# A list-scheduled attention stage: its weight conversions as three vector steps, its table of dates and one tile's path replaced

## The chip, the cores and the metric

The kernel runs on one core of one Trainium2 chip. The metric is the device time of one execution in microseconds (us). The median of three runs before the change is 1078.47 us, and the runs lie between 1077.97 and 1079.72 us. The core has five engines with a queue each: PE (matmul; PEld is its weight load), DVE (vector), ACT (scalar activation), POOL (GpSimd) and SP, which here only issues DMAs. Each works through its queue in order.

## The reference

Three layers follow each other. The first is an attention over 4 batches of 8 heads, 576 positions and 64 channels, whose scores more than tau below the maximum of their row are dropped:

```python
scores = scale * np.matmul(q, k.transpose(0, 1, 3, 2))
thresh = np.max(scores, axis=-1, keepdims=True) - tau
scores = np.where(scores >= thresh, scores, -1000000000.0)
attn = np.exp(scores - np.max(scores, axis=-1, keepdims=True))
x = np.matmul(attn / attn.sum(-1, keepdims=True), v)      # then heads side by side: 2304 x 512
g = x @ w_gate                                            # 512 x 1536
x = (g * sigmoid(g) * (x @ w_val)) @ w_out                # 1536 x 512
out = ((x @ w1) * (x @ w2) @ w3) @ w_out2                 # d_ff 1024
```

The weights arrive as 64-bit floats. The chip reads them as pairs of 32-bit words, and each block of 128 x 512 numbers has to be converted before it can be used.

## The kernel before

**Precision.** Every fp32 operand of a matmul is split into a rounded part (hi) and a rest (lo), and products are sums of two or three matmuls. So every tile that comes out of a matmul is evacuated from PSUM twice.

**Attention.** The heads are taken in 16 pairs (p), each with 9 score tiles (i) of 128 x 576. For a tile n, PE multiplies into one of two buffers `s_bank` (L627). DVE reads it twice: E with the row minimum (L659) and the mask into P (L675, which needs E's statistic). ACT takes a small bias step (L668) and the exponential (L684). The matmul of tile n needs the mask of tile n-2, since there are two buffers. Then P is transposed on PE (L591) into one of four `t_bank` buffers, in ten tiles per pair, and each of them is split into hi and lo in `AT` or `ATL` along a path that a letter of `ROWS` gives:

- Y: ACT copies the bank to `tmp` (L801), POOL rounds it (L371) and subtracts (L376). Seven of the ten tiles.
- X: ACT rounds from the bank (L814), DVE subtracts (L818).
- Z: ACT rounds (L814), PE subtracts the rounded part in the bank by a product with minus the identity (L598, function `less`), ACT copies the rest (L825).

The value products (L869, L881) use these tiles. Besides this, each pair transposes and splits the q and k of the next (`khi`, `klo`, `qhi`, `qlo`, L736 and L742), and POOL splits v (`sp`). Every fourth pair POOL also splits leftover rows of q and k (`qkls`) and of v (`VLZ`).

**Weight conversions in attention.** In pairs 3, 6 and 9 (`EARLY`) one block of weights is converted on the side by `plan_conv`. DVE separates the mantissa (L412, L415, L418: three instructions in one step called `begin`), ACT makes the power of two from the exponent (L426, L427), POOL subtracts (L432), DVE forms the value (L444), ACT rounds it (L481) and POOL or DVE takes the rest (L485). The raw weights are fetched by SP (L401), in `begin`, in `value` and in a step of their own.

**What sets the order.** `Plan` is a list scheduler that runs when the program is built. Every step has an engine, two costs (`busy`, how long it holds its engine, and `until`, when its result is there), the steps that it depends on, and a due date in units of score tiles. `Plan.order` puts, engine by engine, the step that can start first, and among those that could start together the one with the earliest date. The dates are offsets from the pair's first tile, taken from the table `W`; `W["two"]` pulls the odd tile of two forward. The result is a fixed order of instructions; nothing is decided on the chip. At the end of attention a second planner (`Program`, from the function `ending` on) orders the last pair and all that follows, beginning from the times at which the first plan ended.

**After attention** come the blocks of `x` and the dense layers, nearly all of it matmuls on L1524 and L1724.

Of the kernel before, what the change touches and what calls it, by code (L numbers as in the profile page):

```python
# [11 lines left out]
I32 = mybir.dt.int32  # L12
U16 = mybir.dt.uint16
ACTF = mybir.ActivationFunctionType
ALU = mybir.AluOpType
# [17 lines left out]
EARLY = (3, 6, 9)  # L33


ROWS, LAST = ("YXYYYXYYYZ",), "XXYZ"

W = {
    "s": 1.84, "two": 0.59, "exp": -0.21, "bias": 2.86, "k": 0.01, "q": 0.5, "left": 4.95,
# [3 lines left out]
}  # L43


# [254 lines left out]
def kernel(  # L300
# [17 lines left out]
    nc = tc.nc  # L318
# [13 lines left out]
    f32 = lambda ap: ap.bitcast(F32)  # L332
# [28 lines left out]
    def tmp(dt=F32):  # L361
        return stg.tile([P, 512], dt, tag="tmp", name="tmp", bufs=N_TMP)
# [21 lines left out]
    wide = 2 if w_gate.dtype == mybir.dt.int64 else 1  # L384
# [19 lines left out]
    def conv_mantissa(raw):  # L404

        if wide == 1:
            return raw
        two = raw.rearrange("p (n t) -> p n t", t=2)
        a, x = two[:, :, 0], two[:, :, 1]
        low = raw.bitcast(U16).rearrange("p (n t) -> p n t", t=4)[:, :, 1]  # L410
        m = tmp(I32)
        nc.vector.tensor_scalar(  # L412
            out=m, in0=x, scalar1=(1 << 20) - 1, scalar2=None, op0=ALU.bitwise_and
        )
        nc.vector.tensor_scalar(  # L415
            out=x, in0=x, scalar1=-(1 << 20), scalar2=None, op0=ALU.bitwise_and
        )
        nc.vector.scalar_tensor_tensor(  # L418
            out=f32(m), in0=low, scalar=2.0 ** -16, in1=m, op0=ALU.mult, op1=ALU.add
        )  # L420
        return a, m, x
# [50 lines left out]
    conv_in, conv_raw, conv_mid = deque(), deque(), deque()  # L472
# [48 lines left out]
    def attention(actx):  # L521
# [6 lines left out]
        ld = lctx.enter_context(tc.tile_pool(name="ld", bufs=2))  # L528
# [184 lines left out]
        plan = Plan()  # L713
# [405 lines left out]
        def plan_conv(due, engine, deps):  # L1119
            k, r = {}, plan.res("tmp")  # L1120

            def begin():
                conv_fetch()
                k["raw"], *k["rest"] = conv_raw.popleft()
                k["bits"] = conv_mantissa(k["raw"])

            def value():
                conv_fetch()
                k["val"] = conv_value(k["bits"])

            def copy():
                k["lo"] = k["rest"][0](k["val"], later=True)

            ld = plan.add("SP", 0.55, 5.0, deps, conv_fetch, due - 4)
            a = plan.add("DVE", 2.8, 2.9, [ld], begin, due, opens=r)
            c = plan.add("ACT", 1.5, 1.65, [a], lambda: conv_power(k["bits"]), due + 0.2)
            d = plan.add("POOL", 1.0, 1.05, [c], lambda: conv_less(k["bits"]), due + 0.4)
            e = plan.add("DVE", 1.0, 1.1, [d], value, due + 1)
            f = plan.add("ACT", 0.47, 0.6, [e], copy, due + 1.2)
            plan.add(engine, 1.25, 1.3, [f], lambda: k["lo"](), due + 1.4, closes=r)  # L1140

# [2 lines left out]
        def make_plan():  # L1144
            score, tops, mask, ex = {}, {}, {}, {}
            es, pv, ready, left_done = {}, {}, {}, {}
            ready[0], second, first_read, lefts[0], vls[0] = plan_start()
            for p in range(NP):
                z = p * NTILE
                tail_pair = p == NP - 1  # L1150
                for i in range(NTILE if not tail_pair else 2):
                    n = z + i
                    deps = [mask.get(n - 2)] + ready[p]
                    if i == 0:
                        deps = deps + [u for t in range(NTILE) for u in pv.get(("T", p - 2, t), [])]
                    if i >= 4 and p == 0:
                        deps = deps + second
                    big = (1.06 if i == 4 else 0.53)

                    def go(n=n):  # L1160
                        banks[n] = mm_scores(*tiles[n])

                    score[n] = plan.add("PE", big, big + 0.17, deps, go, n - W["s"])
                    if tail_pair:
                        continue
                    war = pv.get(("T", p - 2, i), [])

                    def mx(n=n):
                        es[n] = el_max(*tiles[n], banks[n])

                    two = n - n % 2 * W["two"]
                    a = plan.add("DVE", 0.68, 0.91, [score[n]], mx, two)
                    tops[n] = a
                    mask[n] = plan.add(
                        "DVE", 0.73, 0.82, [a] + war,
                        lambda n=n, p=p, i=i: el_mask(p, i, banks.pop(n), es.pop(n)), two + 0.2)
                    group = next(g for g in SETS if i in g)
                    if i != group[-1]:
                        continue
                    c = plan.add(  # L1180
                        "ACT", 0.16, 0.3, [tops[z + j] for j in group],
                        lambda p=p, group=group: el_bias(p, group), n + W["bias"])
                    for j in group:
                        ex[z + j] = plan.add(
                            "ACT", 0.77, 0.79, [mask[z + j], c], lambda p=p, j=j: el_exp(p, j),
                            z + j + W["exp"])
                if tail_pair:
                    break
                if p + 2 < NP:
# [5 lines left out]
                    ld = plan.add("SP", 1.4, 5.0, [mask[z - 1]] if p else [first_read], loads, z)  # L1195
                    landed[p + 2, 0] = landed[p + 2, 1] = ld
                q = p + 1
# [19 lines left out]
                for c in range(4):  # L1217
                    a, e = plan_T(
                        p, z + W["T0"] + W["t0"] * c, row[c], P0, old[:2],
                        lambda c=c, p=p: [pbuf[p, t][:, c * P:(c + 1) * P] for t in range(4)],  # L1220
                        (AT[0][:, 0, c, 0:512], AT[0][:, 1, c, 0:512]))
# [3 lines left out]
                a, lq = plan_T(  # L1225
                    p, z + W["lq"], row[4], [ex[z + 4]], old,
                    lambda p=p: [pbuf[p, 4][:, c * P:(c + 1) * P] for c in range(4)],
                    tuple(ATT[:, :, e, :, 512:S].rearrange("p h c q -> p c h q") for e in range(2)),
                    "p (c h q) -> p c h q")
                uses[4] += a  # L1230
                a, co = plan_corner(p, z + W["co"], [ex[z + 4]], old)
                uses[4] += a
                late = p == NP - 2
                if late:
# [3 lines left out]
                a, kl = plan_T(  # L1238
                    p, z + W["kl"], row[5], P0 + P1, old,
                    lambda p=p: [pbuf[p, t][:, 512:640] for t in range(4)],  # L1240
                    (ATL[:, 0, 0:512], ATL[:, 1, 0:512]))
# [749 lines left out]
    for f in range(PLAIN, NF1):  # L1991
# [3 lines left out]
        one, two = (seven(pair, f, "gv", True, h_dram, "h") for pair in range(2))  # L1995
# [122 lines left out]
    for c in range(NF2 // 2):  # L2118
        t = whole_back(c, -14.0 + 2 * c, first)
# [63 lines left out]
    for at, j in enumerate(order):  # L2183
        c0, n = blocks[j]
# [3 lines left out]
        for t in range(n // P):  # L2188
            bank, a = buf("T"), buf("tmp")
# [57 lines left out]
```

## Time and profile before

| | |
|---|---|
| median of the runs | 1078.47 us (1077.97 to 1079.72) |
| the profiled execution, its own time | 1076.61 us |
| its span, first to last instruction | 1074.8 us |
| PE busy | 1044.9 us, 97% |
| weight loads on PE (PEld) | 910.8 us, 85% |
| DVE | 846.2 us, 79% |
| ACT | 638.7 us, 59% |
| POOL | 285.7 us, 27% |
| mean granted TensorE clock | 0.995 of full speed |

The shares are averages over stages that differ. POOL has almost no work after the first 345 us, and it is the attention stage, up to about 295 us, where all four engines are nearly full at once. There a stage's own rows must be read, not the page's totals.

### The profile page before, as it was taken

The page shows a single profiled execution, that of the slowest core. Times are in us where ns is not written, and L with a number is a line of the kernel's source. Part 1 is how long each engine was busy: PE and PEld are TensorE (multiplying, and loading weights), DVE is VectorE, ACT ScalarE, POOL GpSimd, SP SyncE. Part 2 cuts the span into 40 slices and gives each one's busy share as a digit, 9 for nine tenths or more (in the row PEclk, how much of TensorE's full clock was granted, in tenths as well). Part 3 has the DMA queues.
Part 4 walks back from the last instruction along what each step waited for, and adds up shares of the span by engine and source line. Part 5 has one row for each costly group of instructions (what it writes and reads, how often), then busy time and mean ns, then how long its engine had stood idle before and what let it go on. Part 6 is the DMA issues. An engine that isn't in the chain of part 4 may idle for free.

```text
span 1074.8 us, 16990 instructions
## 1 busy us (share of the span) xinstructions
PE 1044.9 (97%) x5830; PEld 910.8 (85%) x5830; DVE 846.2 (79%) x1551; ACT 638.7 (59%) x1353; POOL 285.7 (27%) x307
## 2 busy tenths in 40 slices
PE   7998989999999999999999999999999999999998
PEld 6998989899877888888888889878888888888886
DVE  8999999999997969999999975976977776442320
ACT  6998989999874546665667654544433444232220
POOL 5899898998854000000000000000000000000000
PEclk9999999999999999999999999999999999999999
DMA  7686866776557124545457661461222325621531
GB/s 181 162 213 172 195 157 161 202 169 155 161 168 255 39 94 161 183 152 206 152 182 238 225 232 41 159 232 40 83 84 89 123 92 193 240 79 52 152 121 49
DMA packets 127206, 162.37 MB, mean 151 GB/s; under 512 B 48688, under 2 KB 83312, under 8 KB 127120
## 3 DMA queue, kind: packets, MB, share of 16 engines
q1 hardware_dynamic: 126976, 161.29, 49.4%
q8 instruction: 46, 0.75, 0.3%
q14 instruction: 40, 0.33, 0.1%
q10 hardware_dynamic: 144, 0.00, 0.0%
HBM read 93.47 MB, written 44.19 MB: 128 GB/s over the span
## 4 chain that ended last, share of the span: by engine, by line
PE 78%; DVE 12%; ACT 5%; issue 2%; DMA 2%; SPq 1%; POOL 0%; DVEq 0%; ACTq 0%
PE t_bank L1524 26%; PE t_bank L1724 16%; PE s_bank L1724 11%; PE s_bank L627 6%; PE s_bank L1524 6%; PE t_bank L591 5%; PE t_bank L869 4%; DVE slot L1564 2%; ACT P L684 1%; DVE P L675 1%; DVE E L659 1%; DMA x_dram<-xs 1%; PE t_bank L881 1%; DMA slot<-v_dram 1%; DVE slot L1620 1%
## 5 line engine op out<-in xcount | busy, mean ns | idle before, releaser
L1524 PE MATMUL t_bank<-slot,slot 128*128 128x512 f32 (+1 forms) x1680 | 340.7, 362 | 2.4 <-DVE slot L1564 2.4
L1524 PEld LDWEIGHTS t_bank<-slot,slot 128*128 128x128 f32 x1680 | 285.5, 190 | 53.1 <-DVE slot L1564 4.3
L1724 PE MATMUL t_bank<-slot,slot 128*128 128x512 f32 x816 | 196.8, 390 | 0.6 <-ACT tmp L1743 0.6
L1564 DVE TENSOR_TENSOR slot<-slot,slot 128x512 fp32r<-128x512 f32 (+1 forms) x247 | 158.5, 677 | 40.2 <-ACT slot L2015 28.0
L1724 PEld LDWEIGHTS t_bank<-slot,slot 128*128 128x128 f32 x816 | 152.1, 188 | 32.0 <-ACT tmp L1743 1.4
L1724 PE MATMUL s_bank<-slot,slot 128*128 128x512 f32 x612 | 147.0, 389 | 0.0
L376 POOL TENSOR_TENSOR AT<-tmp,AT 128x512 fp32r<-128x512 f32 x105 | 137.4, 1308 | 8.5
L1724 PEld LDWEIGHTS s_bank<-slot,slot 128*128 128x128 f32 x612 | 114.9, 188 | 23.8
L1743 ACT COPY tmp<-t_bank 128x512 f32<-128x512 f32 x102 | 59.4, 583 | 114.2 <-PE t_bank L1724 114.0
L675 DVE SCALAR_TENSOR_TENSOR P<-s_bank,stat,E 128x576 f32<-128x576 f32 x144 | 114.4, 811 | 2.0
L684 ACT ACTIVATE P<-P,stat 128x576 f32<-128x576 f32 x144 | 112.1, 779 | 3.9 <-DVE P L675 1.6
L659 DVE TENSOR_SCALAR_CACHE_REDUCE E<-s_bank,tau_sb 128x576 f32<-128x576 f32 x135 | 107.0, 810 | 7.4 <-PE s_bank L627 7.1
L1572 ACT CAST slot<-slot 128x512 fp32r<-128x512 f32 x135 | 81.0, 621 | 52.9 <-DVE slot L1564 19.5
L627 PE MATMUL s_bank<-R,L 128*128 128x288 f32 x512 | 95.5, 313 | 13.4 <-DVE P L675 12.3
L627 PEld LDWEIGHTS s_bank<-R,L 128*128 128x128 f32 x512 | 73.1, 190 | 19.3 <-issue 13.1
L591 PE MATMUL t_bank<-ident,P 128*128 128x128 f32 x640 | 88.7, 279 | 0.0
L1524 PE MATMUL s_bank<-slot,slot 128*128 128x512 f32 (+1 forms) x432 | 84.7, 354 | 0.0
L1524 PEld LDWEIGHTS s_bank<-slot,slot 128*128 128x128 f32 x432 | 71.5, 189 | 11.3
L591 PEld LDWEIGHTS t_bank<-ident,P 128*128 128x128 f32 x640 | 76.1, 144 | 2.2 <-DVE AT L1310 0.4
L426 ACT ACTIVATE raw<-raw,ebias 128x512 int32<-128x512 int32 x76 | 58.9, 775 | 30.7 <-DVE slot L1614 30.7
L2015 ACT CAST slot<-slot 128x512 fp32r<-128x512 f32 (+1 forms) x100 | 52.7, 577 | 37.4 <-DMA slot<-h_dram 32.7
L869 PE MATMUL t_bank<-AT,sp 128*128 128x288 f32 x448 | 73.9, 298 | 0.0
(157 smaller groups left out, 1330.9 us busy)
## 6 DMA issues: line engine op xcount, KB each, us to landing
slot<-h_dram SPq DMA_DIRECT2D x40, 512.0 KB
h_dram<-h SPq DMA_DIRECT2D x34, 512.0 KB
raw<-in_moe_w_dram SPq DMA_DIRECT2D x32, 512.0 KB
raw<-in_moe_w_out_dram SPq DMA_DIRECT2D x20, 512.0 KB
x_dram<-xs SPq DMA_DIRECT2D x64, 144.0 KB
L<-qlo SPq DMA_DIRECT2D x60, 128.0 KB
L<-qhi SPq DMA_DIRECT2D x60, 128.0 KB
raw<-in_moe_w_gate_dram SPq DMA_DIRECT2D x12, 512.0 KB
```

The costliest lines, as they stand in the source:

```text
L376: nc.gpsimd.tensor_tensor(out=lo, in0=src, in1=f32(hi), op=ALU.subtract)
L591: nc.tensor.matmul(bank[:, t * P:(t + 1) * P], lhsT=part, rhs=ident, is_transpose=True, start=(t == 0), stop=(t == len(parts) - 1),)
L627: nc.tensor.matmul(o, lhsT=lhs, rhs=R[:, c:c + HALF], start=(h == hs2[0] and e == 0), stop=(h == hs2[-1] and e == 1),)
L659: nc.vector.tensor_scalar(out=halves(t), in0=sb[:, :, 0:HALF], scalar1=tau_sb, scalar2=None, op0=ALU.add, op1=ALU.min, accum_out=st[:, 0, c],)
L675: nc.vector.scalar_tensor_tensor(out=halves(p_tile(p, i)), in0=sb[:, :, 0:HALF], scalar=st[:, 0, c], in1=halves(t), op0=ALU.is_gt, op1=ALU ...
L684: nc.scalar.activation(out=u, in_=u, func=ACTF.Exp, scale=-FAR, bias=st[:, 1, c], accum_out=sums[p // HP][:, c],)
L869: nc.tensor.matmul(b["t"][:, 0:HALF], lhsT=splits[p, 2][:, 4 * h + c, :, :].rearrange("p a d -> p (a d)"), rhs=AT[h][:, e, c, cs], start=( ...
L1524: nc.tensor.matmul(o, lhsT=lhs(a), rhs=rhs(c), start=(first and i == 0), stop=(last and i == 2))
L1564: nc.vector.tensor_tensor(out=out, in0=x, in1=y, op=ALU.subtract)
L1572: act(lambda: nc.scalar.copy(out=un["t"][:, 0, :], in_=src()), [key], [(un, 0)], 0.52, due, after)
L1724: nc.tensor.matmul(ap(), lhsT=un["t"][:, a, (off + kk) * P:(off + kk + 1) * P], rhs=x[kk]["ap"](c), start=(start and kk == 0 and i == 0), ...
L1743: act(lambda: nc.scalar.copy(out=k[n]["t"], in_=xa()), [(x, 0)], [(k[n], 0)], 0.47, NOW)
```

## The change

`ROWS` puts the second of the ten tiles on path Z, where it was on X. The table `W` gets other numbers throughout. `plan_conv` splits its first step into three with dates 0.05 apart, so that the scheduler can set other steps between them, and gives the value step a larger cost. The score step on DVE (`mx`) gets larger costs too. The instructions of a conversion are the same as before, with new line numbers for the mantissa (L1131, L1138, L1145).

```diff
-ROWS, LAST = ("YXYYYXYYYZ",), "XXYZ"
+ROWS, LAST = ("YZYYYXYYYZ",), "XXYZ"
 W = {
-    "s": 1.84, "two": 0.59, "exp": -0.21, "bias": 2.86, "k": 0.01, "q": 0.5, "left": 4.95,
+    "s": 1.87, "two": 0.47, "exp": 0.37, "bias": 4.36, "k": -1.1, "q": 0.82, "left": 4.25,
...
             def begin():
                 conv_fetch()
-                k["raw"], *k["rest"] = conv_raw.popleft()
-                k["bits"] = conv_mantissa(k["raw"])
+                raw, *k["rest"] = conv_raw.popleft()
...
+                    nc.vector.tensor_scalar(
+                        out=m, in0=x, scalar1=(1 << 20) - 1, scalar2=None, op0=ALU.bitwise_and
+                    )
+
+            def high():
...
+                    nc.vector.tensor_scalar(
+                        out=x, in0=x, scalar1=-(1 << 20), scalar2=None, op0=ALU.bitwise_and
+                    )
+
+            def low():
...
+                    nc.vector.scalar_tensor_tensor(
+                        out=f32(m), in0=k["low"], scalar=2.0 ** -16, in1=m,
+                        op0=ALU.mult, op1=ALU.add,
+                    )
...
-            a = plan.add("DVE", 2.8, 2.9, [ld], begin, due, opens=r)
+            a = plan.add("DVE", 0.7, 0.8, [ld], begin, due, opens=r)
+            a = plan.add("DVE", 0.6, 0.7, [a], high, due + 0.05)
+            a = plan.add("DVE", 1.2, 1.3, [a], low, due + 0.1)
             c = plan.add("ACT", 1.5, 1.65, [a], lambda: conv_power(k["bits"]), due + 0.2)
             d = plan.add("POOL", 1.0, 1.05, [c], lambda: conv_less(k["bits"]), due + 0.4)
-            e = plan.add("DVE", 1.0, 1.1, [d], value, due + 1)
+            e = plan.add("DVE", 1.3, 1.4, [d], value, due + 1)
...
-                    a = plan.add("DVE", 0.68, 0.91, [score[n]], mx, two)
+                    a = plan.add("DVE", 0.73, 1.02, [score[n]], mx, two)
```

What this does to the queues is seen at three places. The first is DVE in the first conversion (pair 3). Before, from the mantissa (L412) to the value (L444):

```order
L412 TENSOR_SCALAR tmp<-raw 128x512
L415 TENSOR_SCALAR raw<-raw 128x512
L418 SCALAR_TENSOR_TENSOR tmp<-raw,tmp 128x512
L659 TENSOR_SCALAR E,stat<-s_bank,tau_sb 128x576
L818 TENSOR_TENSOR AT<-t_bank,AT 128x512
L675 SCALAR_TENSOR_TENSOR P_1022<-s_bank,stat,E 128x576
L659 TENSOR_SCALAR E,stat<-s_bank,tau_sb 128x576
L675 SCALAR_TENSOR_TENSOR P_1023<-s_bank,stat,E 128x576
L659 TENSOR_SCALAR E,stat<-s_bank,tau_sb 128x576
L675 SCALAR_TENSOR_TENSOR P_1024<-s_bank,stat,E 128x576
L444 SCALAR_TENSOR_TENSOR tmp<-tmp,raw 128x512
```

After, the first of the three mantissa steps (L1131) and what follows it:

```order
L1131 TENSOR_SCALAR tmp<-raw 128x512
L818 TENSOR_TENSOR ATL<-t_bank,ATL 128x512
L659 TENSOR_SCALAR E,stat<-s_bank,tau_sb 128x576
L742 SCALAR_TENSOR_TENSOR qlo<-t_bank,q_scale,qhi 128x512
L675 SCALAR_TENSOR_TENSOR P_1018<-s_bank,stat,E 128x576
L659 TENSOR_SCALAR E,stat<-s_bank,tau_sb 128x576
```

and behind that the other two (L1138, L1145), up to the value:

```order
L1138 TENSOR_SCALAR raw<-raw 128x512
L675 SCALAR_TENSOR_TENSOR P_1019<-s_bank,stat,E 128x576
L1145 SCALAR_TENSOR_TENSOR tmp<-raw,tmp 128x512
L659 TENSOR_SCALAR E,stat<-s_bank,tau_sb 128x576 x2
L675 SCALAR_TENSOR_TENSOR P_1015<-s_bank,stat,E 128x576
L675 SCALAR_TENSOR_TENSOR P_1016<-s_bank,stat,E 128x576
L659 TENSOR_SCALAR E,stat<-s_bank,tau_sb 128x576
L444 SCALAR_TENSOR_TENSOR tmp<-tmp,raw 128x512
```

Five steps of other work now stand between the first two mantissa steps and one between the last two. Between the last of them and the value stand five instructions (two of them in one row), where seven stood before.

The second place is ACT in the same conversion. Before, from the exponential of the tile whose mask stands just ahead of the mantissa (P_1026) to the two powers (L426, L427):

```order
L684 ACTIVATE P_1026,sums<-P_1026,stat 128x576
L894 COPY xs<-t_bank 128x288
L801 COPY tmp<-t_bank 128x512
L814 CAST AT<-t_bank 128x512
L801 COPY tmp<-t_bank 128x512 x2
L426 ACTIVATE raw<-raw,ebias 128x512
L427 ACTIVATE raw<-raw,ebias 128x512
```

After, from the exponential of the tile whose mask stands just ahead of the last mantissa step (P_1019):

```order
L684 ACTIVATE P_1019,sums<-P_1019,stat 128x576
L426 ACTIVATE raw<-raw,ebias 128x512
L427 ACTIVATE raw<-raw,ebias 128x512
L801 COPY tmp<-t_bank 128x512
L814 CAST AT<-t_bank 128x512
L801 COPY tmp<-t_bank 128x512
```

The powers now follow that exponential at once; a value copy (L894) and four evacuations stood between before. On POOL the subtraction L432 stands behind the split of v (`sp`) now, where it stood between the round and the subtraction of a tile.

The third place is DVE in a pair without a conversion (the last pair but two, behind its `qlo`). Before:

```order
L659 TENSOR_SCALAR E,stat<-s_bank,tau_sb 128x576 x2
L675 SCALAR_TENSOR_TENSOR P_4016<-s_bank,stat,E 128x576
L675 SCALAR_TENSOR_TENSOR P_4017<-s_bank,stat,E 128x576
L659 TENSOR_SCALAR E,stat<-s_bank,tau_sb 128x576 x2
L675 SCALAR_TENSOR_TENSOR P_4013<-s_bank,stat,E 128x576
L675 SCALAR_TENSOR_TENSOR P_4014<-s_bank,stat,E 128x576
L818 TENSOR_TENSOR AT<-t_bank,AT 128x512
L659 TENSOR_SCALAR E,stat<-s_bank,tau_sb 128x576 x2
L675 SCALAR_TENSOR_TENSOR P_4015<-s_bank,stat,E 128x576
L675 SCALAR_TENSOR_TENSOR P_4016<-s_bank,stat,E 128x576
L659 TENSOR_SCALAR E,stat<-s_bank,tau_sb 128x576
L675 SCALAR_TENSOR_TENSOR P_4306<-s_bank,stat,E 128x576
```

After:

```order
L675 SCALAR_TENSOR_TENSOR P_4013<-s_bank,stat,E 128x576
L659 TENSOR_SCALAR E,stat<-s_bank,tau_sb 128x576
L675 SCALAR_TENSOR_TENSOR P_4014<-s_bank,stat,E 128x576
L659 TENSOR_SCALAR E,stat<-s_bank,tau_sb 128x576
L675 SCALAR_TENSOR_TENSOR P_4010<-s_bank,stat,E 128x576
L659 TENSOR_SCALAR E,stat<-s_bank,tau_sb 128x576
L675 SCALAR_TENSOR_TENSOR P_4011<-s_bank,stat,E 128x576
L659 TENSOR_SCALAR E,stat<-s_bank,tau_sb 128x576
L675 SCALAR_TENSOR_TENSOR P_4012<-s_bank,stat,E 128x576
L659 TENSOR_SCALAR E,stat<-s_bank,tau_sb 128x576
L675 SCALAR_TENSOR_TENSOR P_4013<-s_bank,stat,E 128x576
L659 TENSOR_SCALAR E,stat<-s_bank,tau_sb 128x576
```

E and P of single tiles alternate now where two E stood ahead of two P, and the subtraction L818 into AT is gone (it is L598 on PE and L825 on ACT now). The last 935 rows of PE's queue, the dense layers, are the same in both.

## Rows read from the trace of the kernel before

**Rows 1.** Windows: start:end, length, busy (count) PE, PEld, DVE, ACT, POOL, PEclk, DMA.
```profile
20.00:285.00 265.00, 251.75 (x1933) 242.32 (x1930) 252.34 (x489) 245.00 (x650) 240.17 (x259) 0.99 0.71 173
253.35:270.53 17.18, 17.18 (x137) 16.75 (x136) 16.22 (x34) 16.47 (x45) 14.90 (x16) 1.00 0.64 151
345.00:1074.00 729.00, 723.53 (x3492) 610.42 (x3492) 525.60 (x937) 342.48 (x593) 1.38 (x2) 1.00 0.40 137
```
**Rows 2.** Instructions of tile qlo: min/median/max ns, first and last start.
```profile
L742 DVE SCALAR_TENSOR_TENSOR qlo<-t_bank,q_scale,qhi x15: 730/741/752, 14.0 to 270.5; 128x512 fp32r<-128x512 f32 x15
```
**Rows 3.** Timeline of DVE, qlo: start us, us, line [idle before <-releaser].
```profile
66.65 0.74 DVE L742 SCALAR_TENSOR_TENSOR qlo<-t_bank,q_scale,qhi 128x512 fp32r<-128x512 f32 x1
...
85.72 0.75 DVE L742 SCALAR_TENSOR_TENSOR qlo<-t_bank,q_scale,qhi 128x512 fp32r<-128x512 f32 x1
...
107.09 0.73 DVE L742 SCALAR_TENSOR_TENSOR qlo<-t_bank,q_scale,qhi 128x512 fp32r<-128x512 f32 x1
...
141.86 0.73 DVE L742 SCALAR_TENSOR_TENSOR qlo<-t_bank,q_scale,qhi 128x512 fp32r<-128x512 f32 x1
...
164.29 0.74 DVE L742 SCALAR_TENSOR_TENSOR qlo<-t_bank,q_scale,qhi 128x512 fp32r<-128x512 f32 x1
...
253.35 0.73 DVE L742 SCALAR_TENSOR_TENSOR qlo<-t_bank,q_scale,qhi 128x512 fp32r<-128x512 f32 x1
...
270.53 0.74 DVE L742 SCALAR_TENSOR_TENSOR qlo<-t_bank,q_scale,qhi 128x512 fp32r<-128x512 f32 x1
```
**Rows 4.** Timeline of all engines in the first conversion, 70 to 86 us.
```profile
70.23 0.97 DVE L412 TENSOR_SCALAR tmp<-raw 128x512 int32<-128x512 int32 x1
...
71.67 1.21 DVE L418 SCALAR_TENSOR_TENSOR tmp<-raw,tmp 128x512 f32<-128x512 uint16 x1
...
78.58 1.03 POOL L432 TENSOR_TENSOR raw<-raw 128x512 int32<-128x512 int32 x1
...
79.64 1.74 DVE L444 SCALAR_TENSOR_TENSOR tmp<-tmp,raw 128x512 f32<-128x512 f32 x1 [1.33 <-POOL raw L432]
...
83.86 2.04 PE L627 MATMUL s_bank<-R,L 128*128 128x288 f32 x8 [3.81 <-DVE P L675]
```
**Rows 5.** Timeline of DVE and POOL in the second and third conversion.
```profile
128.40 1.77 DVE L418 SCALAR_TENSOR_TENSOR tmp<-raw,tmp 128x512 f32<-128x512 uint16 x1
...
135.47 1.04 POOL L432 TENSOR_TENSOR raw<-raw 128x512 int32<-128x512 int32 x1
...
186.84 0.68 DVE L418 SCALAR_TENSOR_TENSOR tmp<-raw,tmp 128x512 f32<-128x512 uint16 x1
...
192.08 1.04 POOL L432 TENSOR_TENSOR raw<-raw 128x512 int32<-128x512 int32 x1
```
**Rows 6.** Timeline of DVE in a pair without a conversion.
```profile
260.46 0.69 DVE L818 TENSOR_TENSOR AT<-t_bank,AT 128x512 fp32r<-128x512 f32 x1
261.07 0.81 DVE L659 TENSOR_SCALAR_CACHE_REDUCE E<-s_bank,tau_sb 128x576 f32<-128x576 f32 x1
...
261.80 0.82 DVE L659 TENSOR_SCALAR_CACHE_REDUCE E<-s_bank,tau_sb 128x576 f32<-128x576 f32 x1
...
266.27 0.82 DVE L659 TENSOR_SCALAR_CACHE_REDUCE E<-s_bank,tau_sb 128x576 f32<-128x576 f32 x1 [0.16 <-PE s_bank L627]
...
267.13 0.82 DVE L675 SCALAR_TENSOR_TENSOR P<-s_bank,stat,E 128x576 f32<-128x576 f32 x1
```
**Rows 7.** Timeline of ACT and PE in the same pair.
```profile
266.76 0.59 ACT L801 COPY tmp<-t_bank 128x512 f32<-128x512 f32 x1 [0.38 <-PE t_bank L591]
267.24 0.61 ACT L736 ACTIVATE khi<-t_bank 128x512 fp32r<-128x512 f32 x1
...
254.25 0.49 PE L598 MATMUL t_bank<-AT,minus_r 128*128 128x512 f32 x1
254.59 1.22 PE L869 MATMUL t_bank<-AT,sp 128*128 128x288 f32 x8
```
**Rows 8.** Waits of POOL, 20 to 300 us: us in total, times, longest us.
```profile
POOL AT L371 <- ACT tmp L801: 16.1, 8, 6.2
```

More of the change, by code (lines that the diff above doesn't have):

```diff
@@ L1123, in begin @@
                 conv_fetch()
-                k["raw"], *k["rest"] = conv_raw.popleft()
-                k["bits"] = conv_mantissa(k["raw"])
+                raw, *k["rest"] = conv_raw.popleft()
+                k["bits"] = raw
+                if wide == 2:
+                    two = raw.rearrange("p (n t) -> p n t", t=2)
+                    k["low"] = raw.bitcast(U16).rearrange("p (n t) -> p n t", t=4)[:, :, 1]
+                    k["bits"] = two[:, :, 0], tmp(I32), two[:, :, 1]
+                    _, m, x = k["bits"]
+                    nc.vector.tensor_scalar(
+                        out=m, in0=x, scalar1=(1 << 20) - 1, scalar2=None, op0=ALU.bitwise_and
+                    )
+            def high():
+                if wide == 2:
+                    x = k["bits"][2]
+                    nc.vector.tensor_scalar(
+                        out=x, in0=x, scalar1=-(1 << 20), scalar2=None, op0=ALU.bitwise_and
+                    )
+            def low():
+                if wide == 2:
+                    m = k["bits"][1]
+                    nc.vector.scalar_tensor_tensor(
+                        out=f32(m), in0=k["low"], scalar=2.0 ** -16, in1=m,
+                        op0=ALU.mult, op1=ALU.add,
+                    )
             def value():
```

6 rows, old and new, of the table W are left out of this document.

## The prediction

> **What bounds the kernel now.** I read the windows first, since the page's shares are means over stages. From 345 us on PE is busy for 723.5 of 729 us [rows 1]; its matmuls there are untouched, so a shift of what lies before is passed on one to one. The change acts on attention, where from 20 to 285 us PE, DVE, ACT and POOL are busy for 252, 252, 245 and 240 of 265 us [rows 1]: no engine has more than a tenth to give, and which of them waits changes within a pair.
>
> Next I used the q subtraction, one per pair, as a clock. It comes 15 times from 14.0 to 270.5 us [rows 2], so a pair takes (270.5 - 14.0) / 14 = 18.32 us on average. An undisturbed pair, from 253.35 to 270.53, takes 17.18 us [rows 3]. The difference over 14 intervals is 16.0 us: this is what start and side work cost beyond an even run. The two intervals around the first conversion take 19.07 and 21.37 us, 6.1 us over two undisturbed ones; around the second one interval takes 22.43 us, 5.25 us over [rows 3]. So conversions hold most of the excess.
>
> How a conversion costs this is seen in the timeline [rows 4]. The mantissa begins at 70.23 and ends at 71.67 + 1.21 = 72.88 us. POOL's subtraction starts only at 78.58 and ends at 79.61 us. DVE had reached the value 1.33 us before that and stood; the value then took 1.74 us, and PE stood 3.81 us for the next mask. The wait of 1.33 us on one engine has become 3.81 us on another, because the queues are in order.
>
> In the undisturbed pair PE is busy for all of 17.18 us and its weight loads for 16.75; DVE is busy for 16.22, ACT for 16.47 and POOL for 14.90 us [rows 1]. Unused are 0.43 us of weight loading, 0.96 of DVE, 0.71 of ACT and 2.28 of POOL.
>
> **The undisturbed pairs after the change.** The subtraction that leaves DVE holds it for 261.07 - 260.46 = 0.61 us [rows 6]. It becomes one more ACT copy, 267.24 - 266.76 = 0.48 us, and one more product with minus the identity, 254.59 - 254.25 = 0.34 us of PE [rows 7]. DVE gives back what it gains: E followed by another E starts it after 261.80 - 261.07 = 0.73 us, E followed by its own mask only after 267.13 - 266.27 = 0.86 us [rows 6], since the mask needs E's statistic. In the pair shown seven tiles stand so after the change and two before, so 5 x 0.13 = 0.65 us are added: DVE comes out even. What alternation gives is slack for PE, which has a whole tile's time to refill the other score buffer; two E in a row do without the 0.13 but sometimes wait for the score, as the 0.16 us in [rows 6].
>
> So ACT's room falls from 0.71 to 0.23 us, and PE's by 0.34. The new product also adds a wait: PE stands until ACT has rounded, and behind it in PE's queue are value products and the next score, for which DVE waits. One such tile per pair exists already. Bounds: the pair cannot be much shorter than ACT's 16.47 + 0.48 = 16.95 us; with the copy wholly on the path it is 17.18 + 0.48 = 17.66. I take 17.30, nearer to the measured row because every engine still has a little room: 14 x 0.12 = +1.7 us (ends -3.2 and +6.7).
>
> Here a rule of the Trainium skill weighs against the change. The rows show PE busy without a gap and weight loads at 97.5% of that pair [rows 1]. The skill (Perfetto Trace Analysis, Identifying the Most-Contended Engine) says that matmul busy time misjudges the room left and that weight-load occupancy is the measure. By that rule PE would be the most contended engine here and the new product would be paid in full, 14 x 0.34 = +4.8 us in place of +1.7. Its result is a case of the last rival below, and the rows do not exclude it.
>
> **The conversions after the change.** The instructions are the same, so no work goes. The three mantissa steps, a block of 72.88 - 70.23 = 2.65 us before [rows 4], let score steps through, and the powers follow on ACT after one exponential and not after five copies. POOL is the open part. From the end of the mantissa to the end of its subtraction it took 6.73 us [rows 4], 136.51 - 130.17 = 6.34 us in the second and 193.12 - 187.52 = 5.60 us in the third conversion [rows 5]. DVE now has five steps of about 0.73 us in between, 3.7 us, where seven stood. If POOL is as late as before, DVE stands 3.0 + 2.6 + 1.9 = 7.5 us, against at least 1.33 before: up to +6.2 us. If the earlier powers and the moved POOL split take 3 us off that chain, DVE stands for next to nothing and the stalls behind it go. What must stay is DVE's work, 2.65 + 1.74 = 4.4 us, less the 2 x 0.96 us that two pairs leave free: 2.5 us. The most to gain is thus 6.1 - 2.5 = 3.6 us in the first and 5.25 - 2.5 = 2.75 in the second; of the other 16.0 - 6.1 - 5.25 = 4.65 us, which the third shares with the start and POOL's extra splits, I count 1: 7.4 us. I take 5.0 us, above the middle of the gains, since the masks that PE waited for are now let in between.
>
> A rule of the skill can be set beside this. The mantissa's last step took 1.21, 1.77 and 0.68 us in the three conversions [rows 4, 5], with POOL busy around each. The skill (SBUF — State Buffer, Who interferes with whom) says that DVE and GpSimd lock one port pair for a whole instruction, a DVE instruction with two SBUF inputs among them, and the later one waits. By that rule each separated step can meet a POOL instruction anew; the spread of 1.1 us once more per conversion would be +3.3 us. Since neither the instructions nor POOL's load change, I leave it at nothing.
>
> SP's fetches stay attached to `begin` and `value` and were issued long ahead, so I cost them at nothing; if one came late it would add a DMA's wait once.
>
> **Sum.** The span is 1074.8 us: + 1.7 - 5.0 = 1071.5. The profiled execution's own time is 1076.6 us, so 1073.3; the median of the runs is 1.9 us above it, which gives 1075.2 us. Against the median this is -0.3%. A change within 0.2%, about 2.2 us, counts as none.
>
> **Rivals.**
> - *Stalls give way almost wholly.* Conversions gain 7.4 us and the pair falls to 17.05 us: 1078.5 - 7.4 - 1.8 = 1069.3. For it: POOL, which has the least choice, waited only 16.1 us in all for its copies, in eight places [rows 8], so most of the 9.2 us can come from feeding it better. Against it: ACT, which feeds it, has the new copy.
> - *The change does not do what it says.* The three steps are spread, but DVE stands at the value as before, since POOL is late and the value stands nearer. Conversions stay where they are and the pairs lose a little or nothing: 1078 to 1080, say 1079. For it: 5.6 to 6.7 us of chain against 3.7 us of cover. Against it: the earlier powers.
> - *Slower: the new tile becomes the bound of every pair.* Each copy of the new tile delays the exponentials behind it, the transposes wait for those, and PE for the transposes. The pair takes 17.66 us, +6.7, and conversions give back only 2: 1083.2. It decides once ACT's own waits per pair exceed the 0.23 us that remain. If only PE's 0.34 us were paid, it would be +4.8 - 2: 1081.3. For it: ACT's room was 0.71 us, and 0.38 us of that was a wait for PE in one place [rows 7]. Against it: alternating scores reach PE earlier.
>
> **Chances.** The forecast 0.42 (its own range 1072.5 to 1077.5), almost wholly gone stalls 0.12, no effect 0.22, the new tile as the bound 0.24. Faster by over 0.2% takes most of the first and all of the second: 0.50; none 0.22; slower 0.28. The range goes from a little under the second case, 1068, to the last, 1083.5.
>
> **What would show it.** In the new profile the q subtractions should lie near 17.3 us apart in pairs without a conversion, and the intervals around a conversion under 20 us. PE's longest wait for a mask should fall from 3.8 to under 2 us. DVE's wait for POOL before the value tells the second rival, and unbroken ACT with pairs of 17.6 us the third. Wrong would be a loss or gain behind 345 us, or at the start.

## The result, and the profile after

The changed kernel takes 1069.46 us (median of 6 runs, 1066.61 to 1073.08), the kernel before 1078.63 beside it (6 runs): ratio 0.9912, 95% interval [0.9892, 0.9933]. The forecast was 1075.2. The profiled execution has a span of 1066.2 us (1074.8 before) and a time of its own of 1068.02 us.

The windows of the profile after, with the columns of [rows 1]; they answer to its three rows:

```profile
20.00:285.00 265.00, 257.26 (x2007) 248.68 (x2006) 254.91 (x494) 256.71 (x683) 245.47 (x262) 1.00 0.72 180
248.21:265.19 16.98, 16.98 (x139) 16.84 (x138) 16.05 (x32) 16.82 (x46) 16.05 (x19) 1.00 0.65 163
345.00:1066.00 721.00, 714.46 (x3445) 601.44 (x3443) 519.82 (x927) 338.97 (x585) 0.00 (x0) 1.00 0.41 137
```

From 20 to 285 us PE is busy 5.5 us more than before and ACT 11.7: more of the work fits into the same time. In a pair without a conversion PE is without a gap, its weight loads fill 16.84 of 16.98 us and ACT 16.82. Behind 345 us little has changed: PE idle for 6.5 us there, 5.5 before. (The window begins at a later point of the work after. Counted from the end, the last 729.8 us hold 3492 matmuls of PE in both.)

The q subtraction after (minimum, median, maximum in ns, first and last start), beside [rows 2]:

```profile
L742 DVE SCALAR_TENSOR_TENSOR qlo<-t_bank,q_scale,qhi x15: 742/748/750, 14.2 to 265.2; 128x512 fp32r<-128x512 f32 x15
```

From the first to the last it is 251.0 us, 256.55 before. The two intervals around the first conversion are 20.0 and 18.2 us (19.07 and 21.37 before [rows 3]), the one around the second 20.3 (22.43). The first conversion, from the timeline of all engines after, beside [rows 4]:

```profile
65.83 1.07 DVE L1131 TENSOR_SCALAR tmp<-raw 128x512 int32<-128x512 int32 x1
...
71.69 1.75 DVE L1145 SCALAR_TENSOR_TENSOR tmp<-raw,tmp 128x512 f32<-128x512 uint16 x1
...
73.47 0.78 ACT L426 ACTIVATE raw<-raw,ebias 128x512 int32<-128x512 int32 x1 [0.49 <-DVE tmp L1145]
...
75.78 0.76 PE L627 MATMUL s_bank<-R,L 128*128 128x288 f32 x4 [1.52 <-DVE P L675]
...
77.20 1.04 POOL L432 TENSOR_TENSOR raw<-raw 128x512 int32<-128x512 int32 x1
...
78.28 1.09 DVE L444 SCALAR_TENSOR_TENSOR tmp<-tmp,raw 128x512 f32<-128x512 f32 x1 [0.87 <-POOL raw L432]
```

From the end of the mantissa (73.44) to the end of POOL's subtraction (78.24) it is 4.8 us, 6.73 before. DVE still stands ahead of the value, 0.87 us. PE's wait for a mask is down from 3.81 to 1.52 us. The steps cost no more for standing apart: over the three conversions the nine mantissa instructions take 8.4 us before and after.

Where the 8.6 us of span come from is best seen between the first q subtraction and the last mask of attention, a stretch with nearly the same matmuls in both. Its windows before and after:

```profile
13.98:299.65 285.67, 268.21 (x2060) 258.26 (x2059) 271.86 (x531) 261.04 (x692) 251.34 (x269) 0.99 0.70 174
```
```profile
14.16:291.63 277.47, 266.32 (x2065) 257.37 (x2064) 265.52 (x513) 265.06 (x704) 251.95 (x269) 0.99 0.72 179
```

It is 8.2 us shorter: PE is idle for 277.47 - 266.32 = 11.15 us in place of 17.46, and busy 1.9 us less. After, 14 more products (L598) of 0.45 us are in it, and 10 value products of the last pair (30 where there were 40) have moved behind the last mask, where ten of them hold PE for about 1.4 us. So not all of the 8.2 us is gained there. Ahead of the stretch 0.2 us are lost, behind it 0.6 gained in spite of these products. The waits in the same stretch (total, times, longest), before and then after:

```profile
POOL AT L371 <- ACT tmp L801: 16.1, 8, 6.2
PE s_bank L627 <- DVE P L675: 15.5, 9, 3.8
ACT tmp L801 <- PE t_bank L591: 9.9, 21, 2.0
DVE E L659 <- PE s_bank L627: 7.1, 21, 0.9
```
```profile
POOL AT L371 <- ACT tmp L801: 12.1, 7, 7.6
PE s_bank L627 <- DVE P L675: 8.8, 9, 2.5
...
DVE E L659 <- PE s_bank L627: 2.9, 4, 1.7
...
ACT tmp L801 <- PE t_bank L591: 2.7, 7, 0.6
```

PE's wait for masks gives 6.7 us, as much as the idle time that went (6.3). ACT and DVE wait less for PE too: with fewer stops anywhere, each of the four engines feeds the next sooner.

A part of PE's busy time is slow matmuls. The profile shows the clock that TensorE was granted, as a share of its full 2.4 GHz. Every stretch up to 400 us in which it was granted its lower level, 1.2 GHz, has a row of windows here: three before, of which the third lies behind the stretch, and one after. The second row after is the place of the first conversion, for comparison:

```profile
84.00:87.50 3.50, 3.50 (x17) 3.48 (x18) 3.50 (x7) 1.45 (x5) 2.89 (x4) 0.52 1.06 296
142.00:145.50 3.50, 3.50 (x19) 3.50 (x19) 2.87 (x7) 1.76 (x3) 3.16 (x6) 0.52 0.96 244
346.50:350.00 3.50, 3.50 (x20) 3.50 (x19) 1.90 (x3) 2.39 (x6) 0.00 (x0) 0.56 0.22 85
```
```profile
16.50:20.00 3.50, 2.75 (x11) 2.78 (x12) 1.78 (x3) 1.75 (x5) 0.00 (x0) 0.54 0.88 213
76.00:79.50 3.50, 3.50 (x28) 3.47 (x28) 2.41 (x5) 3.50 (x10) 3.42 (x4) 1.00 0.69 178
```

Before, PE began 17 matmuls from 84.0 to 87.5 us; after, behind the shorter wait, 28 in as long a time at full clock. A score product (L627) took 427 ns in the first of these windows and 302 in the last. If half of the busy time at the lower clock is what it cost, an estimate, that is 3.5 us in the stretch before and 1.4 after. This fits the 1.9 us, but products were added and moved too, so it is not shown that the clock alone makes them. The first two falls come 0.1 and 1.2 us after PE's waits for a mask in the first and second conversion: 3.81 us up to 83.86 [rows 4], and this one up to 140.76 (timeline of PE before):

```profile
140.76 1.49 PE L627 MATMUL s_bank<-R,L 128*128 128x288 f32 x8 [2.89 <-DVE P L675]
```

The fall that is left after stands at the start, and is new there: from 8 to 16.5 us PE was busy for 4.54 us, 5.25 before. Nor did every long wait bring a fall. Before, PE stood 2.81 us at the start and kept its full clock:

```profile
17.08 1.30 PE L627 MATMUL s_bank<-R,LZ 128*128 128x288 f32 x8 [2.81 <-DVE P L675]
```

So two long waits were paid twice, once in idle time and once in slow matmuls behind them. The Trainium skill (TensorE: Matmul & The Clock Gate, "HAM oscillation — how this bites in real kernels") warns of idle gaps on PE in the middle of a kernel for this reason. The rows of 3.81 and 2.89 us agree; that of 2.81 us does not.

### The profile page after: what moved, and what is told of

Its sections match the earlier page's. It is cut to its first block, busy times and chain, and to the rows that moved or that the text cites. A ratio compares the mean times of both kernels' runs of the same rounds, so it can differ in the third digit from the quotient of the medians.

```text
span 1066.2 us, 16931 instructions
## 1 busy us (share of the span) xinstructions
PE 1042.2 (98%) x5834; PEld 908.4 (85%) x5834; DVE 838.8 (79%) x1536; ACT 644.2 (60%) x1368; POOL 286.4 (27%) x307
## 4 chain that ended last, share of the span: by engine, by line
PE 73%; DVE 12%; ACT 5%; DMA 4%; issue 2%; POOL 2%; SPq 1%; ACTq 0%; DVEq 0%; POOLq 0%
PE t_bank L1549 25%; PE t_bank L1749 16%; PE s_bank L1749 11%; PE s_bank L1549 6%; PE s_bank L627 5%; PE t_bank L591 4%; PE t_bank L869 3%; DVE slot L1589 2%; DVE P L675 2%; ACT P L684 1%; DVE E L659 1%; DMA x_dram<-xs 1%; POOL AT L376 1%; DMA slot<-v_dram 1%; PE t_bank L881 1%
## 5 line engine op out<-in xcount | busy, mean ns | idle before, releaser
L1589 DVE TENSOR_TENSOR slot<-slot,slot 128x512 fp32r<-128x512 f32 (+1 forms) x247 | 155.5, 664 | 41.7 <-ACT slot L2040 28.9
L1749 PEld LDWEIGHTS s_bank<-slot,slot 128*128 128x128 f32 x612 | 114.9, 188 | 23.9
L627 PE MATMUL s_bank<-R,L 128*128 128x288 f32 x512 | 95.4, 308 | 7.9 <-DVE P L675 6.2
L627 PEld LDWEIGHTS s_bank<-R,L 128*128 128x128 f32 x512 | 74.1, 190 | 13.8 <-PE t_bank L591 2.7
L591 PE MATMUL t_bank<-ident,P 128*128 128x128 f32 x640 | 85.3, 273 | 0.4 <-DVE rt L1495 0.4
L426 ACT ACTIVATE raw<-raw,ebias 128x512 int32<-128x512 int32 x76 | 58.8, 774 | 29.4 <-DVE slot L1639 28.8
L591 PEld LDWEIGHTS t_bank<-ident,P 128*128 128x128 f32 x640 | 73.9, 140 | 1.8 <-DVE rt L1495 0.7
```

Of the source, the lines that this page charges most:

```text
L591: nc.tensor.matmul(bank[:, t * P:(t + 1) * P], lhsT=part, rhs=ident, is_transpose=True, start=(t == 0), stop=(t == len(parts) - 1),)
L627: nc.tensor.matmul(o, lhsT=lhs, rhs=R[:, c:c + HALF], start=(h == hs2[0] and e == 0), stop=(h == hs2[-1] and e == 1),)
L1589: nc.vector.tensor_tensor(out=out, in0=x, in1=y, op=ALU.subtract)
L1749: nc.tensor.matmul(ap(), lhsT=un["t"][:, a, (off + kk) * P:(off + kk + 1) * P], rhs=x[kk]["ap"](c), start=(start and kk == 0 and i == 0), ...
```

## The experiments

Twelve kernels were run. Times are medians; ratios are to the kernel before, run beside them. "Stretch" is the one from the first q subtraction to the last mask.

**The parts undone one by one**, and one part alone. First the path letter:

```
-ROWS, LAST = ("YZYYYXYYYZ",), "XXYZ"
+ROWS, LAST = ("YXYYYXYYYZ",), "XXYZ"
```

> The changed kernel with the second tile back on path X; the new table, costs and three steps stay, and the planner orders anew. If the gain of about 9 us lies in the new dates and costs, 1069 to 1073 us, with pairs without a conversion at 17.0 to 17.2 us, since ACT gets 0.48 us of room back. If it lies in the subtraction taken off DVE (15 x 0.61 = 9.2 us), all of it goes: 1077 us or more.

Measured: 1077.09 us, 0.9993 [0.9982, 1.0005]. The whole gain is gone; stretch 288.6 us, longer than before.

The kernel before with the three steps and the conversion's new costs, and nothing else:

```
-            a = plan.add("DVE", 2.8, 2.9, [ld], begin, due, opens=r)
+            a = plan.add("DVE", 0.7, 0.8, [ld], begin, due, opens=r)
+            a = plan.add("DVE", 0.6, 0.7, [a], high, due + 0.05)
+            a = plan.add("DVE", 1.2, 1.3, [a], low, due + 0.1)
```

> The kernel before with the conversion's three steps and its costs, and nothing else. If the block of three mantissa steps is the cause, most of the gain is here: 1070 to 1073 us. If it takes the new dates to use it, the gain is a third or less: 1075 to 1079 us, with pairs without a conversion still at 17.18 us.

Measured: 1083.05 us, 1.0045 [1.0029, 1.0061]: slower. The steps by themselves do not mend the conversion; PE stood 4.14 us there.

The changed kernel with the table of dates of before:

```
-    "s": 1.87, "two": 0.47, ...
+    "s": 1.84, "two": 0.59, ...
```

> The changed kernel with the old table W; path Z, the costs and the three steps stay. If the dates carry the gain, it is lost: 1076 us or more, POOL waiting for ACT's copies 14 us and more as before. If path and steps carry it, 1069 to 1073 us.

Measured: 1077.97 us, 1.0002 [0.9990, 1.0015]. Nothing is left of the gain.

The changed kernel with the conversion in one step, and its old costs:

```
-            a = plan.add("DVE", 0.7, 0.8, [ld], begin, due, opens=r)
-            a = plan.add("DVE", 0.6, 0.7, [a], high, due + 0.05)
-            a = plan.add("DVE", 1.2, 1.3, [a], low, due + 0.1)
+            a = plan.add("DVE", 2.8, 2.9, [ld], begin, due, opens=r)
```

> The changed kernel with the conversion's old form (one mantissa step, the old costs of it and of the value). If the split carries most of the gain, 1076 us or more. By my sum the conversions gained some 4 us over even pairs, so by that 1072 to 1075 us; pairs without a conversion stay at 17.0 us.

Measured: 1078.98 us, 1.0008 [0.9996, 1.0020]. So each of three parts, undone alone, loses all: the path letter, the dates, and the three steps together with the value's cost. The gain cannot be shared out among them, and every theory that gives it to one part falls. The larger costs of the score step were not undone by themselves, and of the parts only the steps were put alone into the kernel before.

**Is it the conversions?** Both kernels in their own order, without the conversions' mantissa, power, subtraction and value. The rounding and the rest that follow read a constant of the same size instead (the edit before, cut):

```
-                k["bits"] = conv_mantissa(k["raw"])
...
-                k["val"] = conv_value(k["bits"])
+                k["val"] = ident[:, 0:1].to_broadcast([P, 512])
...
+            c = plan.add("ACT", 1.5, 1.65, [a], lambda: None, due + 0.2)
+            d = plan.add("POOL", 1.0, 1.05, [c], lambda: None, due + 0.4)
```

> The kernel before, in its own order, with the arithmetic of the three conversions in attention left out (the three mantissa instructions, the two powers, POOL's subtraction and the value); their last rounding and rest read a constant instead. This prices the conversions in the old order. If the stalls at the conversions are most of what the change could win, the intervals around them (19.07 + 21.37, 17.68 + 22.43) fall to 35 to 37 us for two, and the whole to 1068 to 1071 us. If POOL's other side work makes those intervals, they stay above 38 us and the whole above 1072.

> The same left out of the changed kernel, in its own order. If the new order hides the conversions as I summed (5 of 7.4 us won), only 2 to 4 us come off: 1066 to 1068 us. If the gain of the change lies elsewhere, as much comes off as in the kernel before.

Measured: 1071.13 us before, 0.9947 [0.9929, 0.9966], and 1063.76 after, 0.9870 [0.9850, 0.9890]. The change is still worth about 7.4 us with the conversions left out. Their stretches:

```profile
14.47:294.61 280.14, 268.03 (x2070) 257.80 (x2068) 262.00 (x519) 256.80 (x686) 245.58 (x266) 0.99 0.71 177
```
```profile
14.33:288.26 273.93, 266.29 (x2065) 258.96 (x2066) 254.52 (x502) 260.91 (x699) 243.72 (x264) 0.98 0.73 181
```

In the stretch the conversions cost 285.67 - 280.14 = 5.5 us before and 277.47 - 273.93 = 3.5 after: 2.0 of its 8.2 us. The other 6.2 come without them. The interval around the second conversion, 22.43 us before [rows 3], is 22.35 without it, while the one ahead of it falls from 17.68 to 16.02. So the length of the longer one is not the conversion's.

**Which engine sets the pairs now?** ACT's second copy of path Z cut to 128 of its 512 columns (two tiles per pair):

```
-... lambda: nc.scalar.copy(out=lo, in_=b["t"]), ...
+... lambda: nc.scalar.copy(out=lo[:, 0:P], in_=b["t"][:, 0:P]), ...
```

> The changed kernel in its own order; the second copy of each path-Z tile in attention writes 128 of 512 columns (the others stay zero), which takes some 0.3 us from each of two ACT instructions per pair. If ACT, busy 4.97 of 5 us there, is the bound of the pairs without a conversion, they fall from 16.98 us to 16.5 or less and the whole by 4 us or more. If POOL's fixed work sets the time over the whole stage, those pairs fall a little, POOL waits less nowhere, and the whole falls by under 2 us.

Measured: 1068.77 us, 0.9916 [0.9892, 0.9941]: no change. POOL's subtraction of one tile of each pair cut to 128 columns:

```
-... lambda: pool_rest(lo, k["r"], hi), ...
+... lambda: pool_rest(*((t[:, 0:P] if cut else t) for t in (lo, k["r"], hi))), ...
```

> The changed kernel in its own order; POOL's subtraction of the first tile of each pair writes 128 of 512 columns (the others stay zero), some 0.9 us less POOL work per pair. If POOL's work plus its waits is the time of the stage, the last q subtraction comes 4 us or more earlier than at 265.2 us, mostly in the pairs with side work. If ACT or PE sets it, under 1.5 us.

Measured: 1066.08 us, 0.9894 [0.9870, 0.9918]; the stretch falls by 1.8 us to 275.7, while POOL does 251.95 - 239.55 = 12.4 us less in it. The product on PE that takes the rounded part off the bank left out:

```
-d = plan.add("PE", 0.23, 0.45, [c], lambda: less(b["t"], hi), due + W["z"])
+d = plan.add("PE", 0.23, 0.45, [c], lambda: None, due + W["z"])
```

> The changed kernel with the second product of path Z left out in attention (L598, the product that takes the rounded copy off the bank; its rows of L591 and both copies on ACT stay, so that the second copy holds the tile instead of its remainder). The order is the same. In the changed kernel's last two even pairs PE is busy 33.99 of 33.99 us and the chain that ended last is PE alone, ACT is busy 33.57. The two products of a pair take 2 x 0.454 = 0.9 us of PE. If PE sets the even pairs: they fall from 16.98 until ACT's 16.8 stops them, 0.15 to 0.2 us in each, and the whole kernel comes to 1066 to 1068.5. If neither engine alone sets them but the order's hand-overs: they stay at 16.95 to 17.05 and the time at 1069 to 1070.5, as it did when ACT was relieved. If they fall to 16.4 or below, ACT's rows hold idle time that the profile counts as busy.

Measured: 1066.95 us, 0.9901 [0.9888, 0.9915]. Windows of the last pair but one in the three kernels (ACT, POOL, PE relieved), to be set against 16.98 us:

```profile
249.09:266.07 16.98, 16.98 (x138) 16.84 (x138) 16.04 (x32) 16.44 (x46) 16.09 (x19) 1.00 0.61 150
```
```profile
246.59:263.56 16.97, 16.97 (x138) 16.83 (x138) 16.05 (x32) 16.81 (x46) 14.34 (x17) 1.00 0.63 155
```
```profile
247.80:264.64 16.84, 16.78 (x136) 16.44 (x136) 15.93 (x32) 16.68 (x46) 16.17 (x17) 1.00 0.66 165
```

Of these only the pair with less work on PE is shorter, by 0.14 us. But the pair ahead of it in the same kernel is not, 16.99 us in place of 17.01:

```profile
230.81:247.80 16.99, 16.99 (x137) 16.59 (x137) 16.21 (x33) 16.83 (x47) 16.24 (x19) 1.00 0.64 157
```

Over the last three pairs relieving PE gives 0.19 us per pair and relieving POOL 0.08, while relieving ACT gives nothing. What PE was relieved of is two products per pair, about 0.9 us by their own rows. So PE, if any engine, sets these pairs, by a margin of a tenth or two of a microsecond ahead of ACT. Its row reads busy for 16.99 of 16.99 us even with two products less, so a full PE row is not all work. Nothing that is cut from one engine gives more than some 3 us in all, and none of the three ratios is apart from the changed kernel's by its interval.

**Are the dates that fine?** One of the 26 numbers of the table put back:

```
-    "T1": 8.67, ...
+    "T1": 8.3, ...
```

> The changed kernel with one of its 24 dates put back to its old value: T1, the date of the next pair's first turning, 8.3 for 8.67. Costs, steps and paths stay. Theory that the gain belongs to one order that these dates give with these costs: a third of a microsecond in one date moves hundreds of rows, and 3 us or more of the 9 are lost (1072 to 1079). Rival, that the gain belongs to steps, paths and costs, and the dates only have to be near: 1068.5 to 1071.

Measured: 1072.53 us, 0.9947 [0.9930, 0.9964], stretch 280.0 us in place of 277.5. By the medians a third of the gain hangs on this number; the interval just meets that of the changed kernel, so the loss is likely and not certain.

All the planner's costs from the trace, the dates as they are:

```
+            ("POOL", "<lambda>", 0.59): (0.7, 0.7), ("ACT", "<lambda>", 0.16): (0.26, 0.26),
+            ("PE", "<lambda>", 0.23): (0.3, 0.47), ("DVE", "value", 1.3): (1.05, 1.1),
...
+            s["busy"], s["until"] = traced.get(key, (s["busy"], s["until"]))
```

> The changed kernel with the planner's costs of the other steps too set to what the trace shows, its dates unchanged: POOL's rounding of a tile 0.70 (plan 0.59; 102 of them in the stretch), the pair's exponential on ACT 0.26 (plan 0.16; 75), the second product 0.30 (0.23), the conversion's value 1.05 (1.3), its power on ACT 1.62 (1.5), and differences of 0.01 elsewhere. Theory that the plan is better the nearer its costs are to the trace, whatever the dates: first to last qlo falls from 251.0 to 249 to 250.5 and the time to 1066.5 to 1069. Rival, that the dates were found for the costs they stand with, so that any other set loses: 254 us or more between the first and last qlo and 1073 to 1079, as when the parts of the change were undone one by one.

Measured: 1071.40 us, 0.9937 [0.9920, 0.9954], stretch 279.7 us. Truer costs did not make a better order; whether they made a worse one, the intervals leave open. That theory falls; the rival's 1073 to 1079 was not reached either. The same with dates found anew (22 of the 26 differ from the changed kernel's; the expectation has other counts):

```
-    "s": 1.87, "two": 0.47, "exp": 0.37, "bias": 4.36, ...
+    "s": 2.0, "two": 0.43, "exp": 0.71, "bias": 5.52, ...
```

> As the kernel with all costs from the trace, with 18 of the 24 dates found anew for them. Theory that costs and dates have to be fitted together: first to last qlo 248 to 250, time 1065.5 to 1068.5, and not above the one with the old dates. Rival, that the order is at what PE and ACT can do in the even pairs and only the conversions' pairs move: within 1 us of the changed kernel (1068.5 to 1070.5). Rival, that a fit on durations means nothing for the chip: 1073 or more.

Measured: 1073.98 us, 0.9967 [0.9954, 0.9979]. Missed: slower than the changed kernel, as the last rival said.

**What tells all of them apart.** The table sets three things side by side: PE's idle time in the stretch, the time that PE was granted 1.2 GHz up to 400 us (summed over windows of half a microsecond), and the span of the profiled execution. The last column is the span less the idle time and less half of the time at the lower clock.

(The two kernels without conversions do less work and are not in it.)

| kernel | span | PE idle | at 1.2 GHz | remainder |
|---|---|---|---|---|
| before | 1074.8 | 17.5 | 10.2 | 1052.2 |
| after | 1066.2 | 11.2 | 3.4 | 1053.3 |
| path X back | 1077.0 | 19.8 | 13.7 | 1050.4 |
| three steps alone | 1081.6 | 18.7 | 23.9 | 1051.0 |
| old dates | 1079.1 | 16.7 | 20.5 | 1052.2 |
| one step | 1079.6 | 16.7 | 23.9 | 1050.9 |
| ACT relieved | 1067.6 | 10.8 | 10.2 | 1051.7 |
| POOL relieved | 1064.7 | 9.5 | 3.4 | 1053.5 |
| PE relieved | 1065.1 | 13.3 | 6.8 | 1048.4 |
| one date | 1070.8 | 14.3 | 10.2 | 1051.4 |
| all costs | 1072.2 | 12.0 | 13.7 | 1053.4 |
| costs and dates | 1072.8 | 13.8 | 17.1 | 1050.5 |

Spans differ by 17 us, remainders by 5, and by 3.1 without the kernel in which PE does less. Two terms carry nearly all: how long PE stands, and how long it runs slowly. This is close to bookkeeping, since a span is PE's busy time and its idle time; it says where the time goes and not why. Nor is one profile the kernel: the clock differs between executions. The kernel with old dates stands 5.5 us longer than the changed one, and in its profiled execution, slower than most of its 12, is at the lower clock for 17 us more. By the mean granted clock of all runs the clock takes 7.2 us there, 4.6 in the changed kernel and 8.2 in the kernel before (the span times the share of the clock that was not granted, a mean over the runs). So over all runs stops are the larger term there, and of the change's gain the clock is some 3.5 us. Two windows of the kernel with old dates, the third conversion and the passage to the dense layers:

```profile
196.50:200.00 3.50, 3.50 (x18) 3.32 (x17) 3.50 (x7) 1.02 (x4) 2.41 (x3) 0.52 0.91 253
...
309.00:319.50 10.50, 9.50 (x36) 8.58 (x37) 7.50 (x12) 4.71 (x10) 6.61 (x5) 0.51 0.52 154
```

And of the kernel with one step, the start of attention and a fall ahead of which no wait for a mask was over 0.9 us (it began within a wait of 1.88 us, up to 225.81, for POOL's split of v):

```profile
13.00:23.00 10.00, 8.06 (x37) 7.73 (x38) 7.23 (x14) 5.79 (x16) 1.39 (x3) 0.51 0.84 198
...
224.50:231.50 7.00, 5.69 (x24) 5.68 (x25) 1.65 (x4) 1.94 (x6) 3.12 (x4) 0.52 0.35 100
```

This account was formed after the last run, from all the traces. No kernel was made to test it alone, such as one that keeps PE busy with products that nobody uses through the waits of before.

## Why the prediction was right, and where it was off

Faster was right. The size was not: 3 us were forecast and 9 came, the result of the first rival (1069.3), whose own working (7.4 from conversions, 1.8 from pairs) did not come true either. That its number fits is luck.

- **Undisturbed pairs: +1.7 forecast, 14 x (16.98 - 17.18) = -2.8 measured.** This is the term most mis-sized: the choice near the measured row instead of the bound 16.95. I read PE's 17.18 us of busy time as work. Part of it seems to have been stretched matmuls: the score products take 305 ns each in the new pair, 311 in the old. And I counted the 0.16 us of DVE's wait for a score in [rows 6] as a detail; over the pair DVE waited 0.9 us so, and with alternating tiles that is gone. The row of DVE's E in that pair, before and after (busy, mean | idle before):

```profile
L659 DVE TENSOR_SCALAR_CACHE_REDUCE E<-s_bank,tau_sb 128x576 f32<-128x576 f32 x9 | 7.1, 811 | 0.9 <-PE s_bank L627 0.9
```
```profile
L659 DVE TENSOR_SCALAR_CACHE_REDUCE E<-s_bank,tau_sb 128x576 f32<-128x576 f32 x10 | 8.1, 811 | 0.1
```

- **The rule on weight loads** (the Trainium skill, Perfetto Trace Analysis, Identifying the Most-Contended Engine) would have put the pairs at +4.8. It may be right that PE is the most contended: it is the engine whose relief shortened the pairs most. But leaving its two products of 0.45 us out gave 0.19 us per pair, so the product was not paid in full.
- **Conversions: -5.0 forecast.** By the intervals around them it is -4.3 (14.3 us over undisturbed pairs before, 10.0 after), by the kernels without them -2.0 in the stretch. DVE's wait for POOL before the value went from 1.6 us in 2 places to 1.9 in 3, so POOL stayed the late part, as feared. PE's waits for a mask there fell all the same; that the masks let in between did it is argued, not shown alone. The gain was right in kind and mis-sized, and its mechanism was half told: the wait of 3.81 us was followed by a fall of the clock. The sign that was asked for, intervals under 20 us around a conversion, was missed by a little: the longest are 20.0, 20.3 and 20.7 us. The reading under it was wrong too. The 5.25 us by which the second conversion's interval exceeds an undisturbed pair are not the conversion's, since the interval stays at 22.35 us without it. It holds 165 matmuls of PE, where the undisturbed pair holds 137, and PE was busy for 22.36 of its 22.43 us, partly at the lower clock. Conversions did not hold most of the excess: they cost 5.5 us of the stretch. And POOL was not busy around each last mantissa step: it stood from 186.6 to 188.2 us around the third, the one of 0.68 us.
- **A term was missing: the clock.** Two stretches of low clock fewer in the profile, and half of these 6.8 us is 3.4. Over the runs the mean granted clock is 0.9957 after (6 runs) and 0.9924 before (those of all comparisons), which is at most 3.5 us of 1070.
- **The start** was to stay as it was, and did not: the first q subtraction comes 0.2 us later, and the three intervals from it, ahead of the first conversion, take 54.0 us in place of 52.7. There the clock fell anew.
- **"Behind attention one to one"** held within 0.6 us from the last mask on, and in part because terms cancel: more value products stand there, while the fall at 346.5 us is gone. That mask comes 8.0 us earlier, but the last q subtraction only 5.3. The windows from it to the last mask, before and after, show 205 and 192 matmuls of PE, and 10 of the 13 are the value products moved behind the mask. So neither mark is a fixed point of the work:

```profile
270.53:299.65 29.12, 26.77 (x205) 25.80 (x204) 27.78 (x59) 25.15 (x68) 23.40 (x23) 1.00 0.55 154
```
```profile
265.19:291.63 26.44, 25.18 (x192) 24.06 (x190) 25.75 (x54) 23.95 (x65) 22.44 (x23) 1.00 0.59 164
```

- **"Does not do what it says"** is excluded by PE's longest wait for a mask in a conversion, 1.52 us and under 2 as asked. (At the start it waited 2.5 us.) **"The new tile as the bound"** is excluded by pairs of 16.98 us, not 17.6; ACT is nearly unbroken, but relieving it gave nothing.

## What to carry to other kernels

When engines hand work round in a ring, a list order is one fitted whole: cost its parts together, and do not expect a part, truer costs or a looser engine to bring its share. For a stall of TensorE look at the granted clock in the windows just after it, and over several executions, before saying what its removal is worth. And take as the measure of such a stretch PE's idle time between two ends, and count the matmuls between them, since the planner may move the ends themselves.

## What was not expected of the hardware

The granted clock fell to half behind stalls inside attention, not only at the start: behind waits of 3.81 and 2.89 us before, but not behind 1.52 us after. The length of the wait does not decide it alone: a wait of 2.81 us at the start of the kernel before brought no fall, one of 2.27 us with the old dates did, at 84.0 us. In another kernel it fell after several shorter waits (the fall at 224.5 us above: in the 7 us ahead of it PE was busy for 4.5). Runs of one and the same kernel differ by it too: the six of the changed kernel go from a span of 1064.8 us at a mean granted clock of 0.998 to 1071.3 at 0.992.
